# Attention in front of a mixture of experts: heads as separate small score matmuls, a mask added by a matmul, units of a head pair over 16 blocks

## The chip, the cores and the metric

The kernel runs on one core of a Trainium2 chip, in one launch. The metric is the device time of the launch in microseconds. Five engines work side by side, each with its own instruction stream: TensorE (PE in the profile, PEld for its weight loads), VectorE (DVE), ScalarE (ACT), GpSimd (POOL) and SyncE (SP, which here only issues DMAs).

## The reference

Local and global attention for 8 batches of 8 heads, followed by a mixture of 8 experts over the 4608 tokens. Each expert takes exactly 576 tokens, in the order of the logits.

```python
batch, n_heads, seq_l, seq_g, head_dim = (8, 8, 512, 32, 64)
# attention
s_g = scale * q_g @ [k_g, k_l].T;  out_g = softmax(s_g) @ [v_g, v_l]
mask = abs(pos[:, None] - pos[None, :]) <= 32
s_ll = where(mask, scale * q_l @ k_l.T, -1e9)
s_l = concat([scale * q_l @ k_g.T, s_ll]);  out_l = softmax(s_l) @ [v_g, v_l]
# experts (N, D, E, F = 4608, 512, 8, 1024)
logits = x @ w_gate
# greedy over the sorted logits, at most N // E tokens for an expert, one expert for a token
out[mask] = relu(x[mask] @ w1[e]) @ w2[e]
```

All inputs and the output are fp32. The routing depends on the order of the logits, so attention and gate are computed with fp32 matmuls.

## The kernel before, in words

The program is written out in the order in which each engine runs it (`manual_schedule`); no planner moves instructions, and waits between engines come from the tiles that they share.

Attention (`attention`) goes through the batches. The host has laid out, for each batch and pair of heads, the transposed queries (`QW` = 544 columns, 512 local and 32 global), the transposed keys cut into 32-wide blocks with the global keys repeated between them, and for each of the 16 query blocks the 128 rows of values that it needs, with a column of ones (`vw`). The two heads of a pair lie in the upper and the lower 64 partitions.

- A `Local` unit is a head pair over 8 of the 16 query blocks. `a` makes the scores S: the queries of both heads stand in one 128 x 64 stationary tile `qz` with zeros beside them (`spread`, L86, copies them there on GpSimd), and one matmul with 128 moving columns (two key blocks or three, and the global keys) gives a block's scores for both heads (L134). `e` adds the mask and takes the row maximum in one VectorE instruction for each pair of blocks (L141), then ScalarE takes exponentials (L145). `c` transposes the probabilities, four blocks of 128 x 128 (L150, tile T), and copies them out of PSUM (`evac`, L251 on ScalarE, L253 on VectorE, three to two). `d` multiplies with the values (L162, tile O), divides by the sum that the column of ones gives, and writes into `xs` (L170).
- A `Glob` unit is the 32 global queries of four heads against all keys: scores (L195), maximum (L201), exponentials with their sums (L210 to L216), six transposes (L224), outputs (L234).
- The gate (`gate_x`, `gate_m`, `gate_l`) transposes a finished batch of `xs` (L259), multiplies with the gate's weights (L265) and transposes the logits back (L274). Its six steps are handed out one by one to units that follow (`extra`).

A batch is 8 `Local` and 2 `Glob` units. Iteration i of the loop issues, in this order, the scores of unit i + 2, the transposes of unit i, the maxima and exponentials of unit i + 2, and the outputs of unit i - 1. Loads are issued on SP's queue four pairs ahead: `q` and `qk` of one pair, `vw` of the pair before it. PSUM has three S buffers, three T and two O, of one bank each.

After attention the kernel searches, expert by expert, for the tokens of the next expert (`Routing`: small matmuls and VectorE) while the experts' two layers run on TensorE (`experts`, L853 and L881).

Of the kernel before, what the change touches and what calls it, by code (L numbers as in the profile page):

```python
# [8 lines left out]
F32 = mybir.dt.float32  # L9
# [10 lines left out]
S = SL + SG  # L20
# [7 lines left out]
NZ = 6  # L28
NP = H // 2
QW = SL + SG  # L30
KW = 27 * 32
BIG = 3.0e38
# [32 lines left out]
def attention(ctx, tc, A, consts, xd, ident, L, nbatch, rt=None):  # L65
# [6 lines left out]
    G = [(b, g) for b in range(nbatch) for g in range(2)]  # L72
    qk, vw, xs = {}, {}, {}

    def load_qk(b, p):
# [7 lines left out]
        def spread(eng):  # L83
            for h in range(2):
                r = slice(64 * h, 64 * h + 64)
                eng.tensor_copy(z[r, :, h, :], q[r].rearrange("p (j i) -> p j i", i=32))  # L86
        return spread
# [6 lines left out]
    qz = [ac.tile([128, QW // 32, 2, 32], F32, name=f"qz{i}") for i in range(NZ)]  # L94
    pg = [ac.tile([128, 6, 128], F32, name=f"pg{i}") for i in range(2)]
    mask = ac.tile([128, 2 * NB, 128], F32, name="mask")
    wg = ac.tile([128, 4, 32], F32, name="wg")
    P = [(b, p) for b in range(nbatch) for p in range(NP)]
# [3 lines left out]
    wt = ps.tile([128, NB, 128], F32, name="T", bufs=3)  # L102
    for _ in range(WARM):
        nc.tensor.matmul(wt[:, 0, :], warm, warm, start=True, stop=True)
    for i in range(NZ):
        nc.gpsimd.memset(qz[i][64:128, :, 0, :], 0.0)
        nc.gpsimd.memset(qz[i][0:64, :, 1, :], 0.0)
# [3 lines left out]
    nc.sync.dma_start(mask.rearrange("p a b -> p (a b)"), A["mask"])  # L111
    nc.sync.dma_start(ident, A["ident"])
    spread1 = load_qk(0, 1)
# [4 lines left out]

    class Local:
        def __init__(s, b, u):  # L120
            s.b, s.q, s.u = b, u // 2, u % 2

        def a(s):
            b, q = s.b, s.q
            z = qz[(b * NP + q) % NZ]
            kw = qk[b, q]
            st = ps.tile([128, NB, 128], F32, name="S", bufs=3)
            s.p = wk.tile([128, NB, 128], F32, name="p", bufs=4)
            s.nm = wk.tile([128, NB], F32, name="nm", bufs=4)
            for c in range(NB):  # L130
                for r in range(2):
                    j = 8 * s.u + 2 * c + r
                    k0 = 32 * ((3 * j + 1) // 2)
                    nc.tensor.matmul(st[64 * r:64 * r + 64, c, :], z[:, j].rearrange("p h i -> p (h i)"),  # L134
                                     kw[:, k0:k0 + 128], start=True, stop=True)
            s.st = st

        def e(s):
            st, nm = s.st, s.nm
# [3 lines left out]
            nc.vector.tensor_scalar(nm, nm, -SCALE, None, op0=ALU.mult)  # L143
            for c in range(NB):
                nc.scalar.activation(s.p[:, c, :], s.p[:, c, :], AF.Exp, bias=nm[:, c:c + 1], scale=SCALE)  # L145

        def c(s):
            t = ps.tile([128, NB, 128], F32, name="T", bufs=3)
            for c in range(NB):
                nc.tensor.transpose(t[:, c, :], s.p[:, c, :], ident)  # L150
            s.pt = wk.tile([128, NB, 128], F32, name="pt", bufs=3)
            evac(s.pt, t)

        def d(s):
            b, q, u = s.b, s.q, s.u
            o = ps.tile([128, 2, 2, D + 1], F32, name="O", bufs=2)
            for h in range(2):
                for k in range(2):
                    for r in range(4):
                        jj = 4 * k + r  # L160
                        lo = 64 * (jj % 2) + 32 * h
                        nc.tensor.matmul(o[32 * r:32 * r + 32, k, h, :], s.pt[:, jj // 2, lo:lo + 32],  # L162
                                         vw[b, q][:, h, 8 * u + jj, :], start=True, stop=True)
            ls = wk.tile([128, 2, 2], F32, name="ls", bufs=4)
            nc.vector.tensor_scalar(ls, o[:, :, :, D], 1e-9, None, op0=ALU.add)  # L165
            nc.vector.reciprocal(ls, ls)
            if q + u == 0:
                xs[b] = wk.tile([128, NB, DM], F32, name="xs", bufs=2)
            dst = xs[b][:, 2 * u:2 * u + 2, 128 * q:128 * q + 128].rearrange("p k (h d) -> p k h d", h=2)
            nc.vector.tensor_tensor(dst, o[:, :, :, 0:D], ls[:, :, :, None].to_broadcast([128, 2, 2, D]),  # L170
                                    op=ALU.mult)
            if q == NP - 1 and u == 1:
                nc.sync.dma_start(ap_of(xd, (b * S + SG) * DM, [[DM, 128], [128 * DM, NB], [1, DM]]), xs[b])

    class Glob:
        def __init__(s, b, g):
            s.b, s.g = b, g

        def a(s):
            b, g = s.b, s.g  # L180
            s.sa = ps.tile([128, 512], F32, name="S", bufs=3)
            s.sb = ps.tile([128, 32], F32, name="S", bufs=3)
            for part in range(2):
                for r in range(2):
                    i = 2 * g + r
                    t = qk[b, i]
                    z = qz[(b * NP + i) % NZ][:, NW].rearrange("p h i -> p (h i)")
                    if part == 0:
                        base = t[:, 64:128]
                        mv = ap_of(base, 0, [list(base.ap[0]), [96, 8], [1, 64]])  # L190
                        dd = s.sa[64 * r:64 * r + 64].rearrange("p (a b) -> p a b", b=64)
                    else:
                        mv = t[:, 32:64]
                        dd = s.sb[64 * r:64 * r + 64]
                    nc.tensor.matmul(dd, z, mv, start=True, stop=True)  # L195

        def e(s):
            b, g = s.b, s.g
            m = wk.tile([128, 8], F32, name="gm", bufs=2)
            s.m = m  # L200
            nc.vector.tensor_reduce(m[:, 0:1], s.sa, axis=AX.X, op=ALU.max)  # L201
            nc.vector.tensor_reduce(m[:, 1:2], s.sb, axis=AX.X, op=ALU.max)
            nc.vector.tensor_scalar(m[:, 2:3], m[:, 0:1], m[:, 1:2], -SCALE, op0=ALU.max, op1=ALU.mult)
            pgt = pg[(b * 2 + g) % 2]
            s.p = pgt
            f = pgt.rearrange("p a b -> p (a b)")
            d0 = f[:, 0:64]
            d1 = f[:, 512:576]
            pd = list(d0.ap[0])
            nc.scalar.activation(ap_of(d0, 0, [pd, [256, 2], [96, 3], [1, 64]]),  # L210
                                 s.sa[:, 0:384].rearrange("p (a b c) -> p a b c", a=2, c=64), AF.Exp,
                                 bias=m[:, 2:3], scale=SCALE, accum_out=m[:, 3:4])
            nc.scalar.activation(ap_of(d1, 0, [pd, [192, 2], [1, 64]]),
                                 s.sa[:, 384:512].rearrange("p (b c) -> p b c", c=64), AF.Exp,
                                 bias=m[:, 2:3], scale=SCALE, accum_out=m[:, 4:5])
            nc.scalar.activation(f[:, 672:704], s.sb, AF.Exp,  # L216
                                 bias=m[:, 2:3], scale=SCALE, accum_out=m[:, 5:6])

        def c(s):
            s.pt = wk.tile([128, 6, 128], F32, name="pgt", bufs=2)  # L220
            for lo, n in ((0, 4), (4, 2)):
                t = ps.tile([128, NB, 128], F32, name="T", bufs=3)
                for k in range(n):
                    nc.tensor.transpose(t[:, k, :], s.p[:, lo + k, :], ident)  # L224
                evac(s.pt[:, lo:lo + n], t[:, :n])

        def d(s):
            b, g = s.b, s.g
            m = s.m
            o = ps.tile([128, D], F32, name="O", bufs=2)  # L230
            for k in range(6):
                for r in range(4):
                    h = 4 * g + r
                    nc.tensor.matmul(o[32 * r:32 * r + 32, :], s.pt[:, k, 32 * r:32 * r + 32],  # L234
                                     vw[b, h // 2][:, h % 2, 3 * k + 1 if k < 5 else 14, 0:D],
                                     start=(k == 0), stop=(k == 5))
# [761 lines left out]
```

## Time and profile before

| | |
|---|---|
| time, median of 3 runs | 787.63 us (785.98 to 790.63) |
| the profiled execution, from first to last instruction | 797.1 us |
| first score matmul to first routing matmul | 5.38 to 237.95 us |
| TensorE, busy over the span | 717.4 us (90%) |
| VectorE, ScalarE, GpSimd, busy | 504.9, 312.6, 319.3 us |
| moved by DMA | 120.42 MB |

The profile is one execution, with times from its first instruction; it is some 9 us longer than the median of the timed runs. Matmuls are pipelined, so that the mean duration of one is longer than its share of the engine's time: for that, steps are read from one start to the next, as the chain of waits does. "Issue" is a time in which an engine waited for nothing that the profile shows. L numbers are lines of the kernel.

### The profile page before, as it was taken

How to read it: one execution, taken by the hardware profiler on the slowest of the kernel's cores; microseconds unless marked ns; L12 is line 12 of the kernel's file. 1: busy time of each engine (PE TensorE's matmuls, PEld its weight loads, DVE VectorE, ACT ScalarE, POOL GpSimd, SP SyncE). 2: the span in 40 equal slices, each digit the busy share in tenths (PEclk: the TensorE clock that was granted, in tenths of full speed). 3: DMA queues.
4: the chain of work that ended last, by engine and by line, in shares of the span. 5: the costliest groups of instructions: out<-in, count | busy, mean ns of one | idle time of the engine just before them, and what ended most of it. 6: DMA issues, size and time to landing. Idle time of an engine off the chain costs nothing.

```text
span 797.1 us, 19772 instructions
## 1 busy us (share of the span) xinstructions
PE 717.4 (90%) x7876; PEld 578.2 (73%) x7876; DVE 504.9 (63%) x1817; ACT 312.6 (39%) x849; POOL 319.3 (40%) x314
## 2 busy tenths in 40 slices
PE   7899999999982599989988988989899789999994
PEld 6677777777751488779668867858877787987973
DVE  6787887778776888579668667876875752121210
ACT  4656675756640143144223333332331323433410
POOL 5221111111000362566546655563653654574610
PEclk9999999999995579999999999999999999999998
DMA  9998889878310430601430440350341323332000
GB/s 354 406 342 295 327 296 318 314 261 313 142 69 1 145 123 1 264 35 34 143 135 28 150 157 18 120 178 28 120 162 44 119 57 123 132 119 87 28 20 36
DMA packets 32412, 120.42 MB, mean 151 GB/s; under 512 B 6720, under 2 KB 6976, under 8 KB 24128
## 3 DMA queue, kind: packets, MB, share of 16 engines
q1 hardware_dynamic: 22080, 67.78, 23.2%
q0 software_dynamic: 10240, 51.39, 18.6%
q8 instruction: 62, 1.02, 0.5%
q14 instruction: 30, 0.25, 0.1%
HBM read 101.32 MB, written 17.83 MB: 149 GB/s over the span
## 4 chain that ended last, share of the span: by engine, by line
PE 76%; DVE 14%; issue 3%; DMA 3%; POOL 1%; ACT 1%; another core or an unknown queue 0%; POOLq 0%; SPq 0%; ACTq 0%; DVEq 0%
PE Y L881 20%; PE H L853 19%; PE S L134 8%; PE R L468 6%; PE O L162 5%; PE T L150 4%; DVE r_G L405 3%; PE H L726 3%; PE S L195 2%; PE T L259 2%; DVE r_ce L405 2%; PE O L234 2%; PE T L224 2%; PE Y L871 2%; DMA w1r<-in_w_dram,widx 1%
## 5 line engine op out<-in xcount | busy, mean ns | idle before, releaser
L853 PE MATMUL H<-xh,w1h 128*128 128x272 f32 x512 | 153.4, 300 | 9.3 <-DVE hl L405 9.3
L853 PE MATMUL H<-xl,w1h 128*128 128x272 f32 x512 | 152.9, 299 | 0.0
L853 PE MATMUL H<-xh,w1l 128*128 128x272 f32 x512 | 152.5, 298 | 0.0
L405 DVE SCALAR_TENSOR_TENSOR hl<-H,hh 128x272 fp32r<-128x272 f32 x128 | 55.2, 435 | 90.4 <-ACT hh L855 59.7
L145 ACT ACTIVATE p<-p,nm 128x128 f32<-128x128 f32 x256 | 82.0, 394 | 67.5 <-DVE ls L165 34.7
L855 ACT ACTIVATE hh<-H 128x272 fp32r<-128x272 f32 x128 | 51.0, 398 | 145.7 <-PE H L853 138.8
L853 PEld LDWEIGHTS H<-xh,w1h 128*128 128x128 f32 x512 | 100.0, 195 | 10.6 <-DVE hl L405 10.2
L881 PE MATMUL Y<-w2h,hh 128*128 128x512 f32 x256 | 105.6, 412 | 0.0
L704 POOL TENSOR_TENSOR w2l<-w2r,w2h 128x512 fp32r<-128x512 f32 x64 | 82.0, 1304 | 58.8 <-ACT w2h L703 55.8
L704 POOL TENSOR_TENSOR w1l<-w1r,w1h 128x512 fp32r<-128x512 f32 x60 | 78.3, 1321 | 66.3 <-ACT w1h L703 66.1
L881 PE MATMUL Y<-w2h,hl 128*128 128x512 f32 x256 | 104.5, 408 | 0.0
L881 PE MATMUL Y<-w2l,hh 128*128 128x512 f32 x256 | 104.3, 407 | 0.0
L853 PEld LDWEIGHTS H<-xl,w1h 128*128 128x128 f32 x512 | 100.0, 195 | 0.3
L853 PEld LDWEIGHTS H<-xh,w1l 128*128 128x128 f32 x512 | 100.1, 195 | 0.0
L86 POOL COPY qz<-q 64x544 f32<-64x544 f32 x60 | 38.4, 639 | 151.6 <-DMA q<-in_qk_dram 118.5
L826 ACT ACTIVATE y<-Y 128x512 f32<-128x512 f32 (+1 forms) x40 | 23.1, 594 | 134.7 <-PE Y L881 83.1
L134 PE MATMUL S<-qk,qz 128*64 128x128 f32 x1024 | 70.5, 279 | 4.9 <-DVE qz L86 2.8
L134 PEld LDWEIGHTS S<-qk,qz 128*64 128x64 f32 x1024 | 54.9, 136 | 17.4 <-issue 11.3
L733 POOL DMA_INDIRECT out_dram<-y,idx x40 | 41.5, 1036 | 61.6 <-ACT y L826 29.7
L141 DVE CUSTOM_DVE_ANT_0 p<-S,mask 128x128 f32<-128x128 f32 x256 | 58.8, 286 | 6.4 <-PE S L134 4.5
L881 PEld LDWEIGHTS Y<-w2h,hh 128*128 128x128 f32 x256 | 49.2, 192 | 13.9 <-issue 4.2
L703 ACT ACTIVATE w1h<-w1r 128x512 fp32r<-128x512 f32 x64 | 38.3, 627 | 47.1 <-DMA w1r<-in_w_dram,widx 47.1
(165 smaller groups left out, 1273.1 us busy)
## 6 DMA issues: line engine op xcount, KB each, us to landing
vw<-in_vw_dram SPq DMA_DIRECT2D x32, 1040.0 KB, 8.3
qk<-in_qk_dram SPq DMA_DIRECT2D x32, 432.0 KB, 5.8
q<-in_qk_dram SPq DMA_DIRECT2D x32, 272.0 KB, 5.6
xd<-xs SPq DMA_DIRECT2D x8, 1024.0 KB, 7.1
xd<-xg SPq DMA_DIRECT2D x64, 8.0 KB, 5.9
xg<-xd,idx POOLq DMA_INDIRECT x40
out_dram<-y,idx POOLq DMA_INDIRECT x40
mask<-in_mask_dram SPq DMA_DIRECT2D x1, 512.0 KB, 5.7
```

Source lines behind the costliest of these rows:

```text
L86: eng.tensor_copy(z[r, :, h, :], q[r].rearrange("p (j i) -> p j i", i=32))
L134: nc.tensor.matmul(st[64 * r:64 * r + 64, c, :], z[:, j].rearrange("p h i -> p (h i)"), kw[:, k0:k0 + 128], start=True, stop=True)
L141: nc.vector.tensor_tensor_reduce(s.p[:, c, :], st[:, c, :], mask[:, 4 * s.u + c, :], 1.0, -BIG, ALU.add, ALU.max, nm[:, c:c + 1])
L145: nc.scalar.activation(s.p[:, c, :], s.p[:, c, :], AF.Exp, bias=nm[:, c:c + 1], scale=SCALE)
L162: nc.tensor.matmul(o[32 * r:32 * r + 32, k, h, :], s.pt[:, jj // 2, lo:lo + 32], vw[b, q][:, h, 8 * u + jj, :], start=True, stop=True)
L405: return op(*args, **kw)
L468: s.nc.tensor.matmul(out, *args, **kw)
L704: eng.tensor_tensor(lo, raw, hi, op=ALU.subtract)
L733: nc.gpsimd.indirect_dma_start(out=out, out_offset=bass.IndirectOffsetOnAxis(ap=rt.idx[ph][:n, t:t + 1], axis=0), in_=y[:n], in_offset=None)
L853: nc.tensor.matmul(p, w[d][:, fs], x[:, d, q], start=(d + k == 0), stop=(d + k == 5))
L855: nc.scalar.activation(hh[:, f, q], p, AF.Relu)
L881: nc.tensor.matmul(p, h[:, f, q], w[f], start=(f + k == 0), stop=(f + k == 9))
```

## The change

All of it is in attention and in what the host lays out for it; routing and experts are not touched.

- The scores are made for each head by itself: 32 queries of a head (64 partitions by 32 columns) are the stationary operand, read straight from the loaded tile. Each block has one matmul with 96 moving columns (its three key blocks) and one with 32 (the global keys), for each of the two heads. The zero-filled `qz` and `spread` go; in their place the queries are scaled by `-SCALE` where they lie.
- The mask is no longer added by VectorE. Before the scores, one bf16 matmul for each head writes a band of 3e37 and zeros into the columns of the two outer key blocks, and the score matmuls add to it. VectorE takes the row minimum of four blocks in one instruction, and the exponentials read PSUM directly.
- A unit is a head pair over all 16 blocks. A batch is 4 `Local` and 2 `Glob` units; a `Glob` unit is one head of each pair.
- The keys lie once, without repeated global blocks: one load of 1152 columns (576 KB) takes the place of `q` and `qk` (704 KB).
- PSUM: S has two buffers of two banks, T two of one, O one of two.
- The order in an iteration changes, and so do the places of the gate's steps.

The core of the diff:

```diff
     def load_qk(b, p):
-        t = ld.tile([128, KW], F32, name="qk", bufs=5)
-        q = ld.tile([128, QW], F32, name="q", bufs=3)
-        z = qz[(b * NP + p) % NZ]
-        nc.sync.dma_start(q, A["qk"][b, p, :, :QW])
-        nc.sync.dma_start(t, A["qk"][b, p, :, QW:])
+        t = ld.tile([128, QW + KW], F32, name="qk", bufs=7)
+        nc.sync.dma_start(t, A["qk"][b, p])
         qk[b, p] = t
...
+        return lambda eng: eng.tensor_scalar(t[:, :QW], t[:, :QW], -SCALE, None, op0=ALU.mult)
     def load_v(b, p):
-        t = ld.tile([128, 2, NW, D + 1], F32, name="vw", bufs=6)
+        t = ld.tile([128, 2, NW, D + 1], F32, name="vw", bufs=7)
...
     class Local:
         def a(s):
-            st = ps.tile([128, NB, 128], F32, name="S", bufs=3)
-            for c in range(NB):
-                for r in range(2):
-                    j = 8 * s.u + 2 * c + r
-                    k0 = 32 * ((3 * j + 1) // 2)
-                    nc.tensor.matmul(st[64 * r:64 * r + 64, c, :], z[:, j].rearrange("p h i -> p (h i)"),
-                                     kw[:, k0:k0 + 128], start=True, stop=True)
+            s.st = ps.tile([128, 2, NB, 128], F32, name="S", bufs=2)
+            rows = [slice(64 * h, 64 * h + 64) for h in range(2)]
+            for h in range(2):
+                o = s.st[:, h].rearrange("p c (k i) -> p c k i", i=32)[:, :, 0:3:2]
+                nc.tensor.matmul(o, mb[rows[h], 256:384], band[rows[h]], start=True, stop=True)
+            for c in range(NB):
+                for lo, n, k in ((0, 96, None), (96, 32, QW + 576)):
+                    for r in range(4):
+                        j = 4 * c + r
+                        k0 = QW + 32 * j if k is None else k
+                        for h in range(2):
+                            nc.tensor.matmul(s.st[32 * r:32 * r + 32, h, c, lo:lo + n],
+                                             t[rows[h], 32 * j:32 * j + 32], t[rows[h], k0:k0 + n],
+                                             start=False, stop=True, skip_group_check=True)
...
-            for c in range(NB):
-                nc.vector.tensor_tensor_reduce(s.p[:, c, :], st[:, c, :], mask[:, 4 * s.u + c, :], 1.0, -BIG,
-                                               ALU.add, ALU.max, nm[:, c:c + 1])
-            nc.vector.tensor_scalar(nm, nm, -SCALE, None, op0=ALU.mult)
-            for c in range(NB):
-                nc.scalar.activation(s.p[:, c, :], s.p[:, c, :], AF.Exp, bias=nm[:, c:c + 1], scale=SCALE)
+        def m(s):
+            for h in range(2):
+                nc.vector.tensor_reduce(s.nm[:, h], s.st[:, h], axis=AX.X, op=ALU.min)
+        def e(s, h):
+            for c in range(NB):
+                nc.scalar.activation(s.p[h][:, c, :], s.st[:, h, c, :], AF.Exp, bias=s.nm[:, h, c:c + 1], scale=-1.0)
...
     class Glob:
         def a(s):
+            rows = slice(64 * s.g, 64 * s.g + 64)
+            for lo, n, k0 in ((0, 512, QW + 32), (512, 32, QW + 576)):
+                for q in range(NP):
+                    t = qk[s.b, q]
+                    nc.tensor.matmul(s.st[32 * q:32 * q + 32, lo:lo + n], t[rows, SL:QW], t[rows, k0:k0 + n],
+                                     start=True, stop=True)
...
-        if nev[0] % 5 < 3:
+            act = nev[0] % 2 == 0
...
+    for i in range(nu + 1):
...
+        if i + 2 < nu:
+            fetch(units[i + 2])
+        if i < nu:
+            units[i].c(0)
+            if i + 1 < nu:
+                units[i + 1].e(0)
+            units[i].c(1)
+            if i + 1 < nu:
+                units[i + 1].e(1)
+            if i + 2 < nu:
+                units[i + 2].a()
+                units[i + 2].m()
+            units[i].d()
```

`c(h)` transposes one head's four blocks and copies them out, on VectorE for the first head and on ScalarE for the second. `d` multiplies both heads' 16 blocks with the values (32 matmuls), as two units did before. `fetch` issues loads three pairs ahead of unit i + 2. The gate uses T buffers alone.

More of the change, by code (lines that the diff above doesn't have):

```diff
@@ L157, in d @@
+        def d(s):
+            b, q = s.b, s.q
+            o = ps.tile([128, 2, 512], F32, name="O", bufs=1)
             for h in range(2):
-                for k in range(2):
+                for c in range(NB):
                     for r in range(4):
[L160 to L163, printed above, removed]
@@ L179, in a @@
         def a(s):
[L180 to L217, printed above, removed]
@@ L231, in d @@
             for k in range(6):
[L232 to L236, printed above, removed]
-            nc.vector.tensor_reduce(m[:, 6:7], m[:, 3:6], axis=AX.X, op=ALU.add)
-            nc.vector.tensor_scalar(m[:, 6:7], m[:, 6:7], 1e-9, None, op0=ALU.add)
@@ L255, in gate_x @@
-    def gate_x(src, xt, c, spare):
-        t = ps.tile([128, NB, 128], F32, name="S" if spare else "T", bufs=3)
+                for q in range(NP):
+                    nc.tensor.matmul(o[32 * q:32 * q + 32, 0:65], s.pt[:, k, 32 * q:32 * q + 32],
+                                     vw[b, q][:, g, 3 * k + 1 if k < 5 else 14, :], start=(k == 0), stop=(k == 5))
+            m = s.nm
+            nc.vector.tensor_scalar(m[:, 1:2], o[:, D:D + 1], 1e-9, None, op0=ALU.add)
+            nc.vector.reciprocal(m[:, 1:2], m[:, 1:2])
@@ L298, in load_gx @@
         gsrc[i] = t
-    units = []
+    units, at = [], {}
     for b in range(nbatch):
-        loc = [Local(b, h) for h in range(H)]
+        lo = [Local(b, q) for q in range(NP)]
         gl = [Glob(b, g) for g in range(2)]
-        if b < nbatch - 1:
-            us = loc[:4] + [gl[0]] + loc[4:] + [gl[1]]
-        else:
-            us = loc[:2] + gl + loc[2:]
+        us = lo + gl if b < nbatch - 1 else lo[:3] + gl + lo[3:]
+        for k, u in enumerate(us):
+            at[b, "g" if isinstance(u, Glob) else u.q] = len(units) + k
@@ L328, in attention, with fetch @@
     nl = [3]
     def pairidx(u):
-        if isinstance(u, Local):
-            return u.b * NP + u.q
-        return u.b * NP + 2 * u.g + 1
+        return u.b * NP + (u.q if isinstance(u, Local) else NP - 1)
+    def fetch(u):
+        while nl[0] < len(P) and nl[0] <= pairidx(u) + 3:
+            load_qk(*P[nl[0]])(nc.gpsimd)
+            load_v(*P[nl[0] - 1])
+            nl[0] += 1
+            if nl[0] == len(P):
+                load_v(*P[-1])
     nu = len(units)
     first = rt.setup(slice(0, 28)) if rt else None
-    LA = 2
@@ L361, in attention @@
         if rt and i >= nu - 3:
-            for _ in range(6):
+            for _ in range(5):
                 next(first, None)
@@ L919, in experts @@
     force("out")
-def _blocks(a, x, g):
-    pad = np.zeros_like(np.take(x, range(32), axis=a))
-    bl = [pad] + np.split(x, NW, axis=a) + [pad]
-    out = []
-    for i, b in enumerate(bl):
-        out.append(b)
-        if i % 2 == 0 and i < NW + 1:
-            out.append(g)
-    return np.concatenate(out, axis=a)
 def _layout(q_l, k_l, v_l, q_g, k_g, v_g, moe_w_gate, moe_w1, moe_w2):
@@ L946, in _layout @@
     wg[:, :, :E] = moe_w_gate.reshape(4, 128, E).transpose(1, 0, 2)[:, :, ::-1]
-    mask = np.full((128, 2 * NB, 128), 0.0, f)
     i = np.arange(32)
-    for j in range(NW):
-        for w, bk in enumerate([j - 1, j, None, j + 1] if j % 2 else [j - 1, None, j, j + 1]):
-            if bk is not None:
-                t = 32 * bk + i
-                ok = (np.abs(t[None] - 32 * j - i[:, None]) <= 32) & (t >= 0) & (t < SL)
-                for h in (64 * (j % 2), 64 * (j % 2) + 32):
-                    mask[h:h + 32, j // 2, 32 * w:32 * w + 32] = np.where(ok, 0.0, -3.0e37)
+    mask = np.zeros((64, 384), f)
+    band = mask[:, :256].reshape(64, NB, 2, 32)
+    band[:32, :, 0] = np.where(i[None] < i[:, None], BIG, 0.0)[:, None]
+    band[:32, :, 1] = np.where(i[None] > i[:, None], BIG, 0.0)[:, None]
+    band[32, 0, 0] = BIG
+    band[33, NB - 1, 1] = BIG
+    sel = mask[:, 256:]
+    sel[:32] = i[:, None] == np.arange(128)[None] % 32
+    sel[32, :32] = 1
+    sel[33, 96:] = 1
+    mask = np.concatenate([mask, mask])
     p = np.arange(128)
```

197 lines of the change are left out of this document (97 added, 100 removed).

## The prediction

> **What bounds the kernel now.** First part 2 of the page: when the clock and the DMA are full, in 40 slices.
>
> ```profile
> PEclk9999999999995579999999999999999999999998
> DMA  9998889878310430601430440350341323332000
> ```
>
> Attention is the first twelve slices: full clock, DMA near full. Second, busy time by stretch (length, then busy us and instruction count of PE, PEld, DVE, ACT, POOL, then clock, DMA share, GB/s), from the first score matmul at 5.38 to the first routing matmul at 237.95:
>
> ```profile
> 5.38:237.95 232.57, 220.83 (x4572) 163.17 (x4571) 179.91 (x975) 140.57 (x440) 41.91 (x67) 1.00 0.79 289
> 40.00:200.00 160.00, 156.53 (x3284) 116.53 (x3284) 127.17 (x696) 100.57 (x315) 30.69 (x48) 1.00 0.86 308
> ```
>
> TensorE sets the pace; VectorE, next, is busy 77%. Third, the chain in order of time (start, us, what), which gives each step with its change of array shape:
>
> ```profile
> 36.79 1.40 issue
> 44.28 1.09 issue
> 45.37 0.66 PE S L134 x8
> 68.86 1.22 issue
> 110.51 1.10 PE S L195 x8
> 116.60 0.81 PE T L224 x6
> 117.40 0.59 PE O L162 x32
> 117.99 0.86 PE O L265 x8
> 118.85 1.02 PE S L134 x16
> 119.88 0.58 PE T L150 x4
> 120.46 0.81 PE O L234 x48
> 121.27 0.59 PE T L274 x4
> 123.93 1.03 issue
> 124.96 0.42 PE O L162 x13
> ```
>
> A head pair is two units of S 1.02, T 0.58, O 0.59: 4.4 us. A global unit is 1.10 + 0.81 + 0.81 = 2.7, a batch's gate four times 0.58 (its transposes have T's shape) + 0.86 + 0.59 = 3.8. Per batch 4 x 4.4 + 2 x 2.7 + 3.8 = 26.8; eight batches are 214 of the 233 us.
>
> **The odd rows are "issue".** TensorE stops in the middle of a run of O (13 of 32 are left at 124.96) or of S (8 of 16 at 45.37), and waits for no engine. Count the instructions between the ends of such stops:
>
> ```profile
> 31.64:38.18 6.54, 5.14 (x125) 4.12 (x126) 5.34 (x36) 4.32 (x16) 2.56 (x4) 1.00 1.02 404
> 38.18:45.36 7.18, 6.09 (x125) 4.39 (x125) 5.42 (x31) 3.43 (x10) 1.28 (x2) 1.00 1.02 379
> 45.36:70.06 24.70, 23.49 (x504) 17.71 (x504) 19.88 (x114) 16.91 (x53) 5.11 (x8) 1.00 0.91 331
> 70.06:124.95 54.89, 53.85 (x1131) 40.12 (x1130) 43.44 (x236) 33.91 (x108) 10.23 (x16) 1.00 0.86 305
> ```
>
> PE plus PEld: 251, 250, 1008 = 4 x 252, 2261 = 9 x 251. Part 3 of the page has the queue that fits, with packets and MB:
>
> ```profile
> q8 instruction: 62, 1.02, 0.5%
> ```
>
> The 62 packets serve the 15,700 TensorE instructions of the two columns over the span: some 254 each. So q8 brings TensorE's code in blocks of about 252 (256 with its semaphore instructions), and each stop ends where a block begins. The DMA view of single stretches shows when: one packet in 122.74 to 123.68; in 124.96 to 126.09 only data; the next packet in 126.09 to 127.50; in 38.19 to 42.97 only data; in 191.15 to 195.00 only data, then a packet up to 196.00.
>
> ```profile
> q8 instruction: 1, 0.02, 6.2%
> q1 hardware_dynamic: 194, 0.37, 84.5%
> q8 instruction: 1, 0.02, 6.1%
> q1 hardware_dynamic: 523, 1.82, 102.0%
> q1 hardware_dynamic: 307, 1.39, 89.2%
> q8 instruction: 1, 0.02, 6.0%
> ```
>
> The packet was through at 123.68 and TensorE went on at 124.96, 1.3 us later; and the following fetch starts only after TensorE has entered the block just delivered. One block runs, one is on its way, no more. The end of a stop is thus also the request for the next block, and the cycle is a wait behind queued data, about 1 us of transfer, and 1.3 us. Two whole cycles between stops were 6.5 and 7.2 us (DMA share 1.02). In the calmer stage the code asked for at 124.96 was usable at 127.50 + 1.3: 3.8 us; that of 191.15 at 196.0 + 1.3: 6.1 us. The old kernel just escapes: 9143 instructions in 232.57 us are 36 blocks of 6.4 us.
>
> [...]
>
> **The change, part by part.**
>
> *Scores.* Their rows, and those of the outputs:
>
> ```profile
> L134 PE MATMUL S<-qk,qz 128*64 128x128 f32 x1024 | 70.5, 279 | 4.9 <-DVE qz L86 2.8 <-issue 2.2
> L162 PE MATMUL O<-vw,pt 128*32 128x65 f32 x2048 | 43.3, 223 | 3.2 <-issue 2.5 <-ACT pt L251 0.6 <-DVE pt L253 0.2
> ```
>
> 512 score matmuls in the code are 1024 MATMULs, and PEld has as many loads as PE has matmuls: an fp32 matmul is four instructions. A pair's 16 (64 instructions) become 64 small ones (256) and two bf16 band matmuls (4). Execution: O costs 0.81 us for 48 MATMULs (L234, 64 columns) and 0.59 for 32 (L162, 65), so 13.7 ns each, with four column tiles side by side, and 0.15 for the change of shape; T likewise 0.115 each and 0.12. The new ones have 96 or 32 columns, 64 on average, in eight tiles. Upper end: no better than O, 128 x 13.7 ns = 1.75 us. Lower: twice as many abreast, 0.88. I take 0.9, as the tiles of O already run abreast. Band, 256 columns in another shape: at most half an S step, 0.5, at least the 0.15 of a change; I take 0.25.
>
> *Transposes and outputs* keep their number, a pair at a time: O 2 x 0.59 - 0.15 = 1.03, T 2 x 0.58 - 0.12 = 1.04. New pair: 0.9 + 0.15 + 0.25 + 1.04 + 1.03 = 3.4 us against 4.4; six changes of shape become four. Globals and gate execute as before. By execution alone a batch falls from 26.8 to 22.8: eight batches, 32 us.
>
> *Code.* A pair now has, in two units, 32 MATMULs for S, 8 for T and 64 for O, with their loads 208 instructions. After: 260 + 16 + 128 = 404. A global unit goes from 124 to 140 (eight narrow matmuls for four wide). In all 9143 + 32 x 196 + 16 x 16 = 15,670: 62 blocks instead of 36. At 3.4 us a pair a block would last 2.2 us, less than any fetch cycle seen.
>
> *VectorE and ScalarE, per pair.*
>
> ```profile
> L201 DVE TENSOR_REDUCE gm<-S 128x1 f32<-128x512 f32 x10 | 6.8, 684 | 0.9 <-PE S L195 0.9
> L170 DVE TENSOR_TENSOR xs<-O,ls 128x256 f32<-128x256 f32 x41 | 17.4, 424 | 1.4
> L145 ACT ACTIVATE p<-p,nm 128x128 f32<-128x128 f32 x161 | 51.7, 394 | 37.2 <-DVE ls L165 20.6 <-DVE gm L237 9.1 <-DVE nm L143 7.2
> L251 ACT ACTIVATE pt<-T 128x512 f32<-128x512 f32 x26 | 15.4, 591 | 4.9 <-PE T L150 4.9
> ```
>
> VectorE: two 512-wide minima (1.37) for eight fused mask-and-max, a T copy at about the same 0.68, the normalisation at most 2 x 0.42 and two small steps: about 3.1. ScalarE: 8 x 51.7/161 + 0.59 = 3.2. That just fits under 3.4, and easily under a pair that waits for code (1.6 blocks). S, T and O have 2, 2 and 1 buffers instead of 3, 3 and 2: a gate copy queued behind VectorE's normalisation can hold T for about that 0.8 to 1 us, and the next unit's transposes wait for it. I cost this at nothing, since the wait for code covers it; without that cover it is 5 gate steps x 8 x 1 us, 40 us at most.
>
> *Loads.*
>
> ```profile
> vw<-in_vw_dram SPq DMA_DIRECT2D x32, 1040.0 KB, 8.3
> qk<-in_qk_dram SPq DMA_DIRECT2D x32, 432.0 KB, 5.8
> q<-in_qk_dram SPq DMA_DIRECT2D x32, 272.0 KB, 5.6
> ```
>
> 1616 instead of 1744 KB a pair, one issue fewer on SP, one scaling on POOL for two copies (POOL is busy 42 of 233 us): off the path. The write of xs stands in SP's queue ahead of the next loads, as before; seven buffers, three pairs ahead, cover that. The routing's constants are loaded and prepared at about the same point of attention, off the path. The first unit waits for one load of 576 KB instead of 272, about 1 us at 404 GB/s.
>
> **The sum.** A batch is 4 x 404 + 2 x 140 + 56 (gate) = 1952 instructions, 7.7 blocks. The cycle is 6.9 (mean of 6.5 and 7.2) while the DMA is full, that is until seven pairs, 11.6 MB, are loaded at 380 to 404 GB/s: some 30 us. After that I take 4.7: between 3.8 and 6.1 lies 4.95, and the DMA will be less full (7.7 MB a batch, with xs, in 36 us is 215 GB/s against 308). Two blocks are there at the start; the third is asked for at about 6.5 and comes at 13.4, three more bring 34, then 56 x 4.7 = 263, and 8 for the rest. For that rest, the end of attention now, in order of time:
>
> ```profile
> 229.35 0.66 PE L162 MATMUL O<-vw,pt 128*32 128x65 f32 x32 [0.56 <-ACT pt L251]
> ```
>
> From there to 237.95 were 8.6 us of gate steps that wait for each other; they stay. End at 305 against 238: +67. The expert stage is not touched. The profiled execution spans 797.1 us, the timed runs have a median of 787.63; I put the difference on the median: 855 us. With 3.8 throughout: 34 + 213 + 6 (the global units' own execution is longer than that) + 8 = 261, 811 us. With 5.4, halfway between 4.7 and 6.1: 344, 894 us.
>
> **The rivals.**
> - *Code arrives in time*: the buffer is deeper than it seems, or the stops are something else. Execution decides: 787.6 - 32 + 3 (the later start, a longer last unit) = 759; with S at 1.75, 786. For it: most blocks now begin without a stop. Against: the spacing of the stops and the packets after them. It decides if a block comes in under 3.3 us (34 + 7.3 x (6.6 x 3.3 + 5.4) + 8 = 240). [...]
> - *Code at the calmest latency throughout*, 3.3 to 3.5 us: 788 to 798. Against: several loads are queued at once whenever a batch's buffers come free.
> - *The clock falls to half*, as in the slices marked 5. Local blocks hide it, two global units take 10.4 instead of 5.4: 8 x 5 = 40 more, 895. For it: TensorE is idle half the time. Against: the stops of 1.0 to 1.4 us cost no clock.
>
> **How the numbers follow.** Fetch-bound at full clock 0.71, with the clock lost 0.13, calm latency 0.05, code in time 0.11. Slower: the first two and part of the third, 0.86; within 0.5% (4 us, about what a measurement of this kernel can tell) 0.04; faster 0.10. The range 805 to 896 takes the likeliest case between its bounds and most of the lost clock; the cases below it make up most of what is left out.
>
> **What would show it.** Right: "issue" as TensorE's longest wait in attention, stops some 252 instructions apart, about 88 packets on q8 instead of 62, PE and PEld both near half busy, the first routing matmul near 305; S between stops at 0.9 to 1.75 us for 128 MATMULs. Wrong: blocks under 3.3 us, with the end of attention before 238; or PE waiting for VectorE or ScalarE instead; or a 5 in PEclk during attention.

## The result and the profile after

The changed kernel takes 895.3 us against 786.81 for the kernel before: 1.138 times as long, with a 95% interval of 1.132 to 1.144. Of its four runs (893.16, 897.45, 907.36 and 909.03) this counts the two fast ones; the other two, the profiled one among them, are over 1.5% above the fastest, and the median of all four is 902.40. The forecast was 855 (805 to 896): the direction and the cause hold, the size was 40 us short, and the time lies just under the upper bound. The profiled execution spans 907.2 us. In e4 and e5 below, which take nearly as long as the changed kernel (1.140 and 1.142), attention ends at 346 and 344 us; so some 12 of the 358 us discussed next are this execution's own.

First the clock and the DMA share in 40 slices (attention is now the first sixteen), and the page's row of the code queue:

```profile
PEclk8778787887997995559999899999999988999998
DMA  9482626363645401060421433403423331334000
q8 instruction: 87, 1.43, 0.6%
```

Before, PEclk was 9 through all of attention; now it is 7 to 9 (in e4 too; e5's mean is 0.84), and 5 in the last of the sixteen slices, where the gate's last steps wait. The DMA is far from full and comes in bursts. 87 packets of code came instead of 62.

Busy time by stretch, columns as before, from the first score matmul to the first routing matmul, and a stretch in the middle:

```profile
8.11:357.72 349.61, 249.38 (x7702) 189.12 (x7703) 146.06 (x332) 120.24 (x362) 48.62 (x31) 0.82 0.49 178
40.00:200.00 160.00, 113.58 (x3732) 88.66 (x3728) 66.10 (x151) 54.15 (x166) 23.55 (x15) 0.83 0.54 195
```

Attention ends at 357.72 instead of 237.95. TensorE is busy 71% of the middle stretch (98% before), VectorE 41% (79%), and the clock that it is granted is 0.83. Nothing is the bound by its busy time. What TensorE waits for (us in total, times, longest):

```profile
PE S L140 <- issue: 42.7, 19, 5.2
PE O L167 <- issue: 15.6, 7, 3.3
PE O L223 <- issue: 15.1, 5, 5.2
PE T L157 <- DVE xt L117: 6.5, 10, 0.9
PE T L238 <- DMA gx<-xd: 6.3, 1, 6.3
PE T L157 <- issue: 3.4, 1, 3.4
```

76.8 us of "issue" in 32 stops. The chain in order of time, in three places:

```profile
47.37 4.55 issue
...
172.41 1.50 PE S L140 x86
173.91 5.18 issue
179.08 0.32 PE S L140 x5
179.41 1.46 PE O L223 x48
180.86 1.05 PE T L253 x4
...
182.93 0.21 PE S L133 x2
183.14 1.55 PE S L140 x92
...
189.39 1.30 DVE nm L146 x2
190.69 1.54 issue
...
344.44 0.38 SPq L180
...
347.74 2.18 DMA gx<-xd
...
357.38 0.30 DVE L L254
```

A run of scores stops in its middle for 5.18 us. After it the O of a global unit (48 MATMULs) takes 1.46 where it took 0.81 before, and the next four transposes 1.05 where it was 0.58: the clock granted from 179.11 to 182.52 is 0.50 (the last section has the row). The new scores' band (L133) takes 0.21; where a run of scores isn't broken, it is 1.55 us from its first MATMUL to the next step, at full clock. At half clock it is longer: from first start to last end the run at 183.07 takes 1.62 us for its 128 MATMULs, and the 112 ahead of the stop at 28.91, at a granted clock of 0.50, take 2.26:

```profile
26.64 2.26 PE L140 MATMUL S<-qk 64*32 64x96 f32 x112
```

At the end, SP issues the last `gx` loads only behind the store of `xs`.

During the stop at 47.37 the DMA view has

```profile
q1 hardware_dynamic: 487, 1.72, 97.5%
q8 instruction: 1, 0.02, 1.3%
```

one packet of code behind a queue full of data: the pattern of the kernel before, more than three times as often (below).

Adding up the chain's rows by engine, from zero to the first routing matmul, shows where the 120 us are:

| us of the chain in attention | PE | "issue" | VectorE | ScalarE | DMA, SP, POOL | end |
|---|---|---|---|---|---|---|
| before | 210 | 7 | 13 | 1 | 7 | 238 |
| after | 216 | 80 | 38 | 9 | 14 | 358 |

Stops are 72 of the 120 us, VectorE and ScalarE 34, PE 6, the rest 8. TensorE's own part was to fall by 32 us and rose by 6. (What follows attention is untouched: 549 us in this profile, 559 in that of before, 542 to 560 in those of the experiments; so a difference of some us in where attention ends need not show in the time.)

A second count goes along the program. Where a block of 256 instructions begins is known from the order of the instructions (the first four stops behind 10 us come after 446, 699, 954 and 1208 matmuls and weight loads, some 254 apart); its start is that of its first matmul or weight load in the trace, and the matching packet on q8 is known too. In the kernel after, 60 blocks begin in attention. A mean block lasts 5.5 us (before 6.2, with 35 blocks); 33 begin with a stop, some 80 us in all (before at most 10, with under 9 us). Where one stop follows another, a cycle is 5.7 us (3.6 to 8.9): 3.2 from request to packet, 1.0 of transfer, 1.4 from landing to use.

### The profile page after: what moved, and what is told of

Read it like the earlier page. It is cut to its first block, busy times and chain, and to the rows that moved or that the text cites. A ratio compares the mean times of both kernels' runs of the same rounds, so it can differ in the third digit from the quotient of the medians.

```text
span 907.2 us, 25405 instructions
## 1 busy us (share of the span) xinstructions
PE 745.4 (82%) x11140; PEld 604.9 (67%) x11140; DVE 475.1 (52%) x1174; ACT 292.0 (32%) x770; POOL 322.5 (36%) x273
## 3 DMA queue, kind: packets, MB, share of 16 engines
q0 software_dynamic: 10240, 51.39, 16.3%
## 4 chain that ended last, share of the span: by engine, by line
PE 68%; DVE 15%; issue 10%; DMA 2%; ACT 1%; POOL 0%; SPq 0%; POOLq 0%; DVEq 0%; ACTq 0%
PE Y L872 19%; PE H L844 17%; PE S L140 6%; PE R L459 5%; PE O L167 5%; PE T L157 4%; DVE r_G L396 2%; PE S L194 2%; PE T L238 2%; PE H L717 2%; DVE r_ce L396 2%; PE O L223 2%; PE Y L862 1%; PE T L215 1%; DVE nm L146 1%
## 5 line engine op out<-in xcount | busy, mean ns | idle before, releaser
L78 POOL TENSOR_SCALAR qk<-qk 128x544 f32<-128x544 f32 x31 | 48.7, 1570 | 257.2 <-DMA qk<-in_qk_dram 242.0
L146 DVE TENSOR_REDUCE nm<-S 128x4 f32<-128x512 f32 x64 | 41.2, 686 | 115.0 <-PE S L140 115.0
L140 PE MATMUL S<-qk 64*32 64x96 f32 (+1 forms) x4096 | 61.7, 241 | 44.8 <-issue 42.7
L150 ACT ACTIVATE p<-S,nm 128x128 f32<-128x128 f32 x256 | 73.1, 377 | 71.3 <-DVE nm L146 36.8
L140 PEld LDWEIGHTS S<-qk 64*32 64x32 f32 x4096 | 54.3, 115 | 52.9 <-issue 47.3
L157 PE MATMUL T<-ident,p 128*128 128x128 f32 x256 | 50.6, 339 | 11.7 <-DVE xt L117 6.5
```

The costliest lines, as they stand in the source:

```text
L78: return lambda eng: eng.tensor_scalar(t[:, :QW], t[:, :QW], -SCALE, None, op0=ALU.mult)
L140: nc.tensor.matmul(s.st[32 * r:32 * r + 32, h, c, lo:lo + n], t[rows[h], 32 * j:32 * j + 32], t[rows[h], k0:k0 + n], start=False, stop=Tru ...
L146: nc.vector.tensor_reduce(s.nm[:, h], s.st[:, h], axis=AX.X, op=ALU.min)
L150: nc.scalar.activation(s.p[h][:, c, :], s.st[:, h, c, :], AF.Exp, bias=s.nm[:, h, c:c + 1], scale=-1.0)
L157: nc.tensor.transpose(t[:, c, :], s.p[h][:, c, :], ident)
```

## The experiments

All times are medians; ratios are to the kernel before on the same chip, with a 95% interval.

**Is it the number of instructions?** Two kernels: the old one with its score matmuls cut in four, and the changed one with fewer.

```diff
# e1: kernel before
+                for lo in range(0, 128, 32):
...
-                    nc.tensor.matmul(st[64 * r:64 * r + 64, c, :], ..., kw[:, k0:k0 + 128], ...)
+                        nc.tensor.matmul(st[64 * r:64 * r + 64, c, lo:lo + 32], ..., kw[:, k0:k0 + 32], ...)
# e2: changed kernel; keys and values laid out on the host as before
-                for lo, n, k in ((0, 96, None), (96, 32, QW + 576)):
...
+                            nc.tensor.matmul(s.st[32 * r:32 * r + 32, h, c, :], ..., t[rows[h], k0:k0 + 128], ...)
```

> The kernel before, with each score matmul cut into four of 32 columns: the same work, loads, buffers and other engines, only 6144 more TensorE instructions, 15.3 thousand in attention (60 blocks of code instead of 36). Code theory: the end of attention is 60 blocks times a cycle of 5.5 to 6.0 us, 330 to 360 us instead of 238, and the time 880 to 910 us; stops called issue, 252 instructions apart. Rival, execution sets the pace: 128 narrow MATMULs a pair at the 12 ns that the new kernel's score runs show after their first 32 are 1.5 us against 1.74, so 780 to 790 us.

865.60 us, 1.099 (1.090 to 1.108); attention ends at 320. Slower, as the code theory has it, but for another reason in the main: S is 133 us of the chain (63 before), and "issue" 18.

```profile
PE S L135 <- issue: 9.6, 8, 2.1
PE O L163 <- issue: 4.4, 5, 1.5
```

A quarter-wide MATMUL took 33 ns (133 us by 4096) where the whole took 61. So execution nearly made room for the code: blocks of 5.1 us, with some 17 us of stops. Both forecasts were missed, and the run doesn't separate the two causes.

> The changed kernel with the keys and values laid out as before the change, so that one matmul of 128 columns takes the place of the two of 96 and 32: 276 TensorE instructions a pair instead of 404, 11.6 thousand in attention (46 blocks instead of 62), the same columns streamed; the loads grow from 576 to 704 KB of queries and keys a pair. Code theory: 46 blocks at the 5.5 us measured, attention ends near 255 instead of 349, 795 to 825 us. Rival, execution and the buffers between engines set the pace: a run of scores falls by no more than 0.6 us, 32 x 0.6 = 20 us, so 875 to 885 us.

842.71 us, 1.071 (1.064 to 1.077); attention ends at 287.

```profile
PE O L166 <- issue: 16.7, 9, 3.4
PE T L156 <- DVE xt L117: 11.9, 15, 1.1
PE O L236 <- issue: 6.8, 3, 2.8
...
```

Half of the loss is gone, with 16 of the 25 added blocks (44 now, 60 in the changed kernel, 35 before). The stops fell from some 80 to some 37 us. Neither theory's number was met: the code theory had left 7 to 37 us over, and 54 are.

**Is the wait one behind queued data?** The changed kernel with the values of the first batch used throughout, and with two 4-byte DMAs (`pace`) that read the last pair's tiles, so that SP issues a pair's loads only after the last ones have landed.

```diff
# e3
     def load_v(b, p):
+        if b > 0:
+            vw[b, p] = vw[0, p]
+            return
# e4
+            pace(qk[P[nl[0] - 1]], vw[P[nl[0] - 2]])
             load_qk(*P[nl[0]])(nc.gpsimd)
```

> The changed kernel without the loads of values after the first batch (all later batches use those of the first, so the output is another): 30 of 62 MB of attention's transfers go, the instructions stay. Code theory, with the wait behind queued data as the largest part of a cycle: cycles of 3.5 to 4.0 us once the first batch is loaded, attention ends at 235 to 270, 785 to 820 us. Rival, the code's cycle does not depend on the data in the queues, or execution at the lowered clock sets the pace: no change, 885 to 910 us.

883.27 us, 1.122 (1.112 to 1.131): between the two numbers, and far from the theory's.

```profile
PE S L143 <- issue: 29.3, 18, 5.2
PE O L226 <- issue: 18.3, 5, 5.0
PE O L170 <- issue: 14.8, 8, 3.0
```

With the DMA share down to 0.3, stops of 5 us are still there. The cycle between stops fell from 5.7 to 4.9 us only.

> The changed kernel with its loads let out a pair at a time: before each pair's loads SP issues two transfers of 4 bytes that read the tiles loaded before, and so waits until these have landed. At most 1.65 MB are queued ahead of a block of code. Code theory: the mean cycle falls from 5.5 to about 4.7 us, 45 us less, 830 to 880 us. Rival, the wait is not that of queued data: 895 us or more, since loads only come later.

898.95 us, 1.140 (1.133 to 1.148): no gain. So the first form of the theory (all of the wait is data, and spreading it helps) fell.

**Is it the buffers instead?** A gate copy in VectorE's queue holds T; here all gate copies go to ScalarE, in the changed kernel (e5) and in that with merged scores (e6).

```diff
-        evac(xt[:, c, :n * 128], t[:, :n].rearrange("p a b -> p (a b)"))
+        evac(xt[:, c, :n * 128], t[:, :n].rearrange("p a b -> p (a b)"), act=True)
...
-        evac(ltc[:, :n * 128], lt[:, :n * 128])
+        evac(ltc[:, :n * 128], lt[:, :n * 128], act=True)
```

> All gate copies (of a batch's four transposed blocks and of its logits) go to ScalarE; nothing else changes. If the added time is code that comes late, with a clock that falls behind it, only the waits of T for VectorE's gate copy go (6.5 us in ten waits in the changed kernel, some of them covered by the next wait for code): 888 to 903 us, stops for code still 70 to 85 us of the chain. If it is the buffers (a gate copy queued behind VectorE's normalisation, which the prediction bounded at 40 us): 860 to 885 us.

898.72 us, 1.142 (1.136 to 1.148).

```profile
PE S L140 <- issue: 36.1, 18, 4.3
...
```

The waits for VectorE's gate copies are gone and the time is the same. Up to the end of attention VectorE is 16 us of the chain (38 in the changed kernel), ScalarE 17 (9), PE 221 (216). The theory that gate copies cost the time by holding T falls; fewer buffers as such were not tested.

> The changed kernel with merged scores (one 128-column matmul for a block and head, 276 instructions a pair), and its gate copies on ScalarE too. With merged scores alone 842.7 us, T waited 11.9 us for VectorE's gate copies in fifteen waits. Code theory: with a third of the added instructions left the stops cover less, so some of those waits are now on the path: 828 to 840 us. Buffers as the main cause of what is left against the kernel before: 800 to 825 us.

837.93 us, 1.064 (1.059 to 1.070): 5 us less than without, within the code theory's numbers; the two intervals overlap.

**What does code cost by itself?** 1536 one-column fp32 matmuls ahead of the kernel before.

```diff
+    for k in range(1536):
+        r = 32 * (k % 4)
+        nc.tensor.matmul(wt[r:r + 32, 0, 0:1], warm[:, 0:32], warm[:, 0:1], start=True, stop=True)
```

> 1536 one-column fp32 matmuls (6144 instructions, 24 blocks) stand ahead of the kernel before, with next to no work in them; they run while the first seven pairs are loaded (some 30 us) and then with no data queued. By the code theory a block takes 5 to 7 us at first and, with idle queues, its fixed part: 3.3 to 3.8 us (1.0 us of transfer, 1.3 to 1.4 us from landing to use, about 1 us from request to packet), together 24 blocks in 90 to 105 us, 85 to 100 us more than before in the whole. If code is not what TensorE stops for, 6144 instructions go at the 8 to 12 ns that a weight load and its matmul took: 25 to 37 us more.

878.27 us in one run, 92.7 more than before, as the code theory had it. TensorE's timeline, and its busy time by stretch:

```profile
5.62 2.93 PE L107 MATMUL T<-warm 128*32 128x1 f32 x203
12.60 1.88 PE L107 MATMUL T<-warm 128*32 128x1 f32 x128 [4.04 <-issue]
18.80 1.89 PE L107 MATMUL T<-warm 128*32 128x1 f32 x128 [4.31 <-issue]
...
28.45 1.88 PE L107 MATMUL T<-warm 128*32 128x1 f32 x128 [1.57 <-issue]
```

```profile
8.37:25.00 16.63, 3.96 (x269) 3.72 (x264) 0.00 (x0) 0.00 (x0) 4.57 (x8) 1.00 0.98 393
25.00:97.00 72.00, 38.66 (x2615) 37.01 (x2616) 0.00 (x0) 0.00 (x0) 1.28 (x2) 1.00 0.02 5
```

This shows the fetch bare. TensorE stops after exactly 128 MATMULs, that is 256 instructions with their loads, every time. With the DMA full (share 0.98) a block takes 6.2 us, with it empty (0.02) 3.45, sometimes 3.73. (The shortest cycle between stops in the chains of e3 and e11 is nearly that too, 3.46 and 3.55. The score rows that follow speak against the 1.00 in the clock column; see the end.)

**Code and data, two by two.** With the floor known, the changed kernel and that with merged scores, both with all loads left out after the first batch: the values as in e3, and the queries and keys.

```diff
     def load_qk(b, p):
+        if b > 0:
+            qk[b, p] = qk[0, p]
+            return lambda eng: None
```

> The changed kernel with keys, queries and values loaded for the first batch alone; the later batches compute on those, so the output is that of other data, with all of TensorE's instructions kept, and POOL's scaling goes with the loads. Queues then hold only the stores of xs and xg. In code alone a block of 256 took 3.45 to 3.75 us with idle queues and 6.2 us beside the first loads; in the changed kernel a block that had to be waited for took 5.7 us, with values loaded once 4.9. Theory: waiting behind data is the difference, so such blocks now take 3.5 to 4.0 us, the stops fall from 80 to 25 to 40 us, and the whole to 835 to 860 us. Rival: the length of the stops comes from the order of the instructions (dense scores, then chains through VectorE), not from the queues: 870 us or more, as with values loaded once (883).

849.27 us, 1.083 (1.075 to 1.091), within the theory's numbers.

```profile
PE O L173 <- issue: 13.7, 10, 1.9
PE O L229 <- issue: 13.0, 5, 3.5
PE S L146 <- issue: 8.8, 9, 2.3
```

The longest stop is 3.5 us, the sum halved, a mean block 4.6 us.

> The same loads left out of the changed kernel with merged scores (276 instructions a pair in place of 404). Theory: at 3.5 to 4.0 us a block, 44 blocks are 155 to 175 us and no longer set the pace; what is left is execution and the chain through VectorE and ScalarE (57 + 10 us of the chain with loads): stops under 15 us, 795 to 820 us. Rival as above: stops stay at 35 to 40 us, 830 us or more. If even this does not come under the kernel before (788), the added time is not the code alone, and what is left is the order of a pair with two score buffers.

792.21 us, 1.011 (1.005 to 1.018), 3 us below the theory's numbers. No stop for code is among its larger waits any more (5.9 us in all):

```profile
PE T L162 <- DVE xt L123: 12.0, 13, 1.1
PE S L145 <- POOL qk L81: 5.3, 2, 3.5
```

PE is now 132 us of its chain, VectorE and ScalarE 73, DMA, SP and POOL 29. An unbroken run of merged scores, in the chain:

```profile
40.39 1.08 PE S L145 x64
```

| time as a ratio to before | 404 instructions a pair | 276 |
|---|---|---|
| loads as they are | 1.138 | 1.071 |
| loads of the first batch alone | 1.083 | 1.011 |

The two add: 128 instructions a pair cost 0.067 to 0.072 (53 to 56 us) with loads or without; the loads, and the scaling on POOL that goes with them, cost 0.055 to 0.060. Not all of the first is code: an unbroken run of scores is 1.08 us merged and 1.55 cut, and 32 times the difference is 15 us of execution. With both away the stops are nearly gone, and the kernel is still 1.1% behind.

**Does a pair of units at a time help by itself?** The kernel before in the order S S T T O O of two units, and then with the waits that this made moved out of the way (the gate ahead of the outputs, exponentials ahead of the copies of T, outputs one unit later).

```diff
-    for i in range(-LA, nu + 3):
+    for i in range(-LA, nu + 3, 2):
+        two = (i, i + 1)
...
+        for j in two:
+            if 0 <= j < nu:
+                units[j].c()
```

> The kernel before, its instructions unchanged, in the order S S T T O O of two units in place of S T O S T O, the two global units of the last batch a little later. The code per unit stays (9143 instructions over attention, 36 blocks). If TensorE's changes of shape (0.12 to 0.15 us each, three fewer for each two units, 40 such pairs) are on the path, attention loses 40 x 3 x 0.13 = 16 us at most, some of it lost again where blocks of 256 instructions come in under 5.5 us: 772 to 782 us against 788. If VectorE's bursts (two units' mask and maximum in a row) or the code make up for it: 786 to 800 us.

812.17 us, 1.028 (1.023 to 1.034).

```profile
PE O L265 <- DVE ls L165: 12.4, 6, 2.8
...
```

> The kernel before in the order S S T T O O as in the run of pairs (812 us), with the waits mended that cost it: the gate step stands ahead of the outputs (there 12.4 us of waits for the normalisation), the exponentials ahead of the copies of T, the global unit's ahead of the local one's (8.0 us), outputs a further unit later. Execution on TensorE was 221 us there against 231. If these waits were all, attention loses 8 to 14 us: 773 to 782 us. If two units in a row always leave a longer chain through VectorE and ScalarE than TensorE has other work for, 790 to 812 us.

819.11 us, 1.027 (1.022 to 1.031). Both times TensorE executes a little less in attention (219 and 215 us busy against 221 in the kernel before, each counted from 5 us to its own first routing matmul), and both are slower: VectorE and ScalarE make 85 and 97 us of the chain in place of 13. Moving the waits out of the way made others. A typical stretch of the second (chain):

```profile
106.77 0.29 DVE p L141
...
107.83 0.70 DVE pt L253
...
108.58 0.66 PE T L259 x4
```

**Do pauses cost the clock?** The kernel before, with VectorE slowed so that TensorE must pause for other reasons than code.

```diff
+            for _ in range(2):
+                nc.vector.tensor_tensor(idle, idle, idle, op=ALU.max)
             for c in range(NB):
                 nc.vector.tensor_tensor_reduce(...)
```

> The kernel before with two elementwise maxima of a 960-wide tile on VectorE (results unused, about 1 us each) ahead of each of the 64 local units' mask step. VectorE then has some 310 us of work in attention and TensorE, with its code unchanged (36 blocks, now with ample time), must pause, at about the share of busy time that it had in the changed kernel (0.72). If pauses of a microsecond or two are what costs the clock, whatever their cause, the granted clock of attention falls to 0.8 to 0.95 and some runs of four transposes take 1 us in place of 0.58; the whole takes 860 to 885 us either way, VectorE setting the pace. If the lost clock belongs to the waits for code or to the new matmuls, it stays at 1.00.

910.49 us in one run (expected were 860 to 885; each maximum took 1.19 us, not 1).

```profile
50.00:90.00 40.00, 28.75 (x517) 19.88 (x520) 38.51 (x134) 15.62 (x50) 7.07 (x8) 0.91 0.56 208
130.00:170.00 40.00, 29.73 (x562) 20.71 (x562) 38.50 (x134) 17.34 (x54) 5.12 (x8) 0.96 0.54 201
```

TensorE is busy 72 to 74%, as in the changed kernel, and the clock is 0.91 to 0.96, not 0.83: pauses of up to 2.8 us, here mostly waits for VectorE and ScalarE, go with some lost clock too. The changed kernel's, of up to 5.2 us, go with 0.83.

## Why the prediction was right and where it was wrong

*The bound.* Right: TensorE is stopped by its own code, in blocks of 256 (e7: 128 MATMULs with their loads from stop to stop). Behind the changed kernel's stops for code the next packet starts 1.0 us or more after TensorE has gone on, never before it, as if one block ran and one was on its way. The announced signs came: "issue" as the longest wait, stops at block boundaries, 87 packets (88 announced). e7 shows it bare, and e2, e11 and e12 take it away step by step. Other signs did not come as announced: the first routing matmul was at 358 and not near 305, TensorE was busy 71% and not half, and PEclk had a 5, though only at the very end of attention.

*The cycle of 4.7 us is the step that failed on size, and the overlap of VectorE and ScalarE is another.* Attention ended at 358 instead of 305. Of these 53 us, 56 blocks at 5.5 instead of 4.7 are some 45, and the end (below) is 8; some 12 of the whole are this execution's own. The 4.7 was taken between two cycles of the calmer stage, 3.8 and 6.1. Two things were wrong with it. The cycle behind stops was 5.7: though the DMA is idle half of the time, the loads come in bursts, and with all loads gone it is about 4.5. And the 27 blocks without a stop were to take 2.2 us of execution and took 5.2. The prediction had VectorE and ScalarE fit under a pair's 3.4 us and easily under the wait for code, at no cost. They are 47 us of the chain here, and 73 in e12, where hardly a stop is left: so these waits don't come from the stops; the stops cover some of them (about 26 us by this comparison), and the sum had let them cover all. Half clock, in some of these blocks, adds to it. The upper bound, 5.4 throughout, gave 894, and is close to what happened.

*Execution 32 us less* never came to bear. Of the scores: 1.55 us for 128 MATMULs, change of shape included, where 1.05 was taken; within the bounds. That is 16 us of the 32: the eight tiles did not run twice as many abreast as the four of O (12.1 ns a MATMUL, 13.7 in O). Why they did not stays open. A single rate of issue for all sizes isn't the reason, as matmuls of 32 columns go faster than those of 96 (last section). The band was right (0.21). The other half, fewer changes of shape, shows in e9 and e10 as 2 and 6 us less of TensorE's busy time, and is outweighed there by waits for VectorE and ScalarE. The order unit by unit, two units ahead, is what keeps the old TensorE 98% busy.

*The rivals.* "Code arrives in time", 759 to 786, isn't what happened; and e12, which is near to that case, with merged scores, took 792: even nearly without the stops, the change was no gain, since the chain through VectorE and ScalarE takes the place of the stops. "The clock falls" was put as an alternative and came along with the stops: TensorE at 0.82 in attention. Its price isn't shown by a run of its own; PE's part of the chain was forecast at 8 x 22.8 = 182 and was 216, of which the scores explain 16, which leaves some 18 us. That this rival's 895 is the time measured is luck: it put 40 us of half clock on top of blocks of 4.7 us.

*Costed at nothing.* The gate copy that holds T: 6.5 us of waits, and no time that shows when removed (e5). The single scaling on POOL took 1.57 us (L78's mean), 1.59 of it once on the path at the start. The end was missed: the gate's steps were to stay at 8.6 us and took 16.3, both from the start of the last run of O, since the last `gx` loads now stand behind the store of `xs` on SP (6.3 us of waiting); only the stores ahead of the next pairs' loads had been thought of.

Left open: the price of the lost clock, and why a request for code took 2.0 us to its packet in e11 and 1.1 in e7, both with nearly empty queues; the stores of `xs` in e11 are one candidate that was not tested.

## What to carry to other kernels

Count instructions, not only cycles: here TensorE got one block of 256 instructions in 3.5 us with empty DMA queues and in 6.2 with full ones (e7), so a matmul cut in four has to be weighed against code first. The old kernel sat near that (6.2 us a block), and so the change, with some 70% more instructions, was largely decided before any execution time was computed. And waits for other engines are not to be put at nothing because a wait for code stands in the same place: here VectorE and ScalarE were 47 us of the chain with the stops and 73 nearly without them.

## What was not expected of the hardware

- In an unbroken run of scores at full clock, a MATMUL of 96 columns took 12 to 17 ns from one start to the next, with its weight load, and one of 32 columns 6.5 to 10 (12.1 ns for all on average). Merged, one of 128 columns took 14 (64 in 0.89 us from first start to last); in the kernel before, one of 65 columns took 13.7. So from 65 to 128 columns the size hardly counted, though the tiles differ, and at 32 it did. The 13.3 ns of a MATMUL of one column in e7 (128 in 1.69 us from first start to last) can't be set beside these, as the next point shows.
- In e7 the view gives a clock of 1.00 through 23 stops of 1.6 to 4.3 us. The score rows that follow speak against it: 16 MATMULs took 1.98 us at 101.46, nearly twice the 1.02 at 114.38.

```profile
101.46 1.98 PE S L137 x16
...
114.38 1.02 PE S L137 x16
```

- In the profiles before and after, the record of the clock has two values only, 1.00 and 0.50 (0.83 is a mean), and they change at the ends of stretches of 3.41 us. In the changed kernel's attention the clock fell 21 times, each time behind such a stretch in which TensorE was busy 1 to 44% of the time, and never behind one with 48% or more. In the rows below the first is followed by half clock, the second isn't; the third is the half clock behind the stop of 5.18 us. In the kernel before, behind attention, a few stretches don't follow this: the clock also fell behind one of 63% (383.95 to 387.36) and one of 87% (650.19 to 653.60), and stayed behind one of 45% (643.36 to 646.77).

```profile
69.88:73.30 3.42, 1.50 (x25) 1.17 (x25) 1.70 (x5) 1.15 (x4) 0.00 (x0) 1.00 0.01 2
172.28:175.70 3.42, 1.63 (x125) 1.46 (x123) 0.02 (x1) 0.54 (x2) 0.00 (x0) 1.00 1.05 302
179.11:182.52 3.41, 3.41 (x61) 3.17 (x62) 2.19 (x6) 1.14 (x4) 1.57 (x1) 0.50 0.18 72
```
